# Block 0 of a fused attention and SwiGLU kernel: each half's reciprocal root on GpSimd, and two unread products in place of seven

## The chip, the cores and the metric

The kernel runs on one core of a Trainium2 chip. A core has five engines that run their own instruction streams and wait for each other through semaphores: TensorE (PE in the profile; its weight loads are PEld), VectorE (DVE), ScalarE (ACT), GpSimd (POOL) and SyncE (SP), which here only issues transfers. The metric is the device time of one execution in microseconds. The kernel before takes 1024.2 us, the median of three runs between 1023.02 and 1026.13.

## The reference, cut to what matters

```python
kv  = einsum('bhsd,bhse->bhde', k, v)             # 8 batches, 8 heads, 576 tokens, 64 wide
out = einsum('bhsd,bhde->bhse', q, kv)
rms = sqrt(mean(out * out, axis=-1) + 1e-06)      # one per token and head
x   = (out / rms * g_norm) as (4608 tokens, 512)
g   = x @ w_gate                                  # 512 x 1536
y   = (g * sigmoid(g) * (x @ w_val)) @ w_out      # back to 512
```

All of it is float32. The weights arrive as 64-bit words, which the kernel rounds to float32 itself, in pieces of 128 x 512.

## The kernel before, in words

The 4608 tokens are worked in nine blocks of 512 (`blocks`, an `Att` and an `Ffn` object for each). A block's attention gives x, transposed so that the model dimension lies across the partitions; then come the up products with silu, and the down product. While one block's down product runs, the attention of the next is fitted in between its steps (`Ffn.down` and its `fill`). Later blocks save multiplications with sums of sub-blocks (`Quad`, `Up`, `Inner`, `Down`), whose lines L565 and L728 are the bulk of TensorE's work. Block 0 is different: nothing runs ahead of it, its weights are still being loaded and rounded, and its up products are plain (`plain_up`, L1032).

The change is in how block 0 begins, `Att.first`. Its 512 tokens are two halves (i = 0 and 1) of two tiles of 128. The steps are these:

- `turn_q` transposes q on TensorE (L337) and copies it out of PSUM on VectorE (L341) and ScalarE (L339).
- `first_kv` makes kv of the first batch (L248).
- `heads` multiplies q with kv for one half (L361), into two PSUM tiles.
- `squares` squares them on ScalarE (L374) and sums over a head's 64 elements on VectorE (L375) into `z`. One half gives 16 numbers a partition.
- `root` makes 1/sqrt(z/64 + eps) on VectorE, for both halves at once: L381, a first guess from the bits (L384), and three Newton steps of L391, L392 and L393, eleven instructions on 128x32.
- `scale` multiplies the products by it (L113, two instructions a half).
- `turn_x` transposes the result on TensorE (L410), and ScalarE copies it out with the gain (L411) into x.
- `warm` has TensorE multiply something that nobody reads (L496), seven times, between the heads of half 1 and the transposes of x.

In between stands the rounding of the weights. `Words.begin` is ScalarE's absolute value (L146), VectorE's clamp (L147), sign (L152) and combination (L153); `Words.finish` is ScalarE's low part (L160) and VectorE's addition (L162). 36 pieces go through it; a piece's load waits for the buffer of the fourth piece before it, and so for L152 and L160 of that one. `plain_up` for feature group f needs the pieces 2f (gate) and 2f+1 (value) and runs group 0 in two halves of the tokens: the first needs x of half 0, the second x of half 1.

What sets the order on each engine: the framework puts the instructions into an order of its own, and `tc.issue_after` pins an instruction behind another. Each engine then runs its list strictly in order, so that one waiting instruction holds up everything behind it. In this kernel VectorE's list reads, from the sums of half 0: L147, L152, L153 of weight piece 0, sums of half 1, the eleven of the root, scaling of half 0, L162 of piece 0, scaling of half 1, piece 1.

Of the kernel before, what the change touches and what calls it, by code (L numbers as in the profile page):

```python
# [8 lines left out]
F32 = mybir.dt.float32  # L9
U32 = mybir.dt.uint32  # L10
I32 = mybir.dt.int32
OP = mybir.AluOpType
ACT = mybir.ActivationFunctionType

P = 128
# [3 lines left out]
def kernel(  # L19
# [41 lines left out]
    nc = tc.nc  # L61

    B, H, S, D = q.shape
# [7 lines left out]
    NS = DM // P  # L71
# [4 lines left out]
    eps = 1e-6  # L76
# [3 lines left out]
    def pool(name, bufs, **kw):  # L80
        return ctx.enter_context(tc.tile_pool(name=name, bufs=bufs, **kw))

    consts = pool("consts", 1)
    ld_pool = pool("ld", 4)
    st_pool = pool("st", 2)
# [8 lines left out]
    a_psum = pool("a_psum", 1, space=PS)  # L94
    b_psum = pool("b_psum", 3, space=PS)
# [6 lines left out]
    gain = consts.tile([P, 1], F32, name="gain")  # L102
    for u in range(2):
        nc.gpsimd.dma_start(out=gain[u * D : (u + 1) * D], in_=g_norm.rearrange("(d o) -> d o", o=1))

    kvs = [consts.tile([P, NS, D], F32, name=f"kv{i}") for i in range(3)]

# [11 lines left out]
    class Words:  # L119
# [12 lines left out]
        def __init__(self, src, shape):  # L132
            self.raw = ld_pool.tile([P, LD], U32, name="ld")[:, 0 : 2 * BLK]
            dst = self.raw.rearrange("p (a b) -> p a b", a=shape[0])
            self.sent = nc.sync.dma_start(out=dst, in_=src)
            self.shape = shape
            self.begun = False
# [45 lines left out]
    def round_w(name, j):  # L183
        if name == "o":
            dst = wo[:, j : j + 1, :]
        else:
            dst = wviews[name][0][j // 2][:, :, P * (j % 2) : P * (j % 2 + 1)]
        piece = words.pop((name, j))
        if not piece.begun:
            piece.begin()  # L190
        return piece.finish(dst)

    class Att:


        def __init__(self, n):
            self.n = n

            self.cut, half = divmod(n, 2)
            self.split = half * D  # L200
            self.ps, self.z = {}, None
            self.q, self.k, self.v, self.room = [], {}, {}, None
            self.halves = []
            self.quarters = n > 0

        def parts(self, t):

            n, first = self.n, P * t - D * self.n
            if t < self.cut:
                return [(n - 1, S + first, 0, P)]  # L210
            if t == self.cut and self.split:
                return [(n - 1, S - D, 0, D), (n, 0, D, P)]
            return [(n, first, 0, P)]
# [153 lines left out]
        def squares(self, i):  # L367
# [4 lines left out]
            for u in range(2):  # L372
                sq = self.sq[:, 2 * i + u]
                self.squared = nc.scalar.activation(out=sq, in_=self.ps[i][u], func=ACT.Square)  # L374
                self.summed = nc.vector.tensor_reduce(out=self.z[:, i, u], in_=sq, axis=mybir.AxisListType.X, op=OP.add)  # L375

        def root(self, i, k=1):


            z = self.z[:, i : i + k]  # L380
            nc.vector.tensor_scalar(out=z, in0=z, scalar1=1.0 / D, scalar2=eps, op0=OP.mult, op1=OP.add)  # L381
            self.y, a = (st_pool.tile([P, 2, 2, 2, NS], F32, name=x) for x in "ya")
            y, a = self.y[:, i : i + k], a[:, i : i + k]
            nc.vector.tensor_scalar(  # L384
                out=y.bitcast(I32), in0=z.bitcast(I32), scalar1=-0.5, scalar2=float(0x5F3759DF),
                op0=OP.mult, op1=OP.add,
            )
            flat = lambda t: t.rearrange("p i u t j -> p (i u t j)")
            y, a, z = flat(y), flat(a), flat(z)
            for _ in range(3):  # L390
                nc.vector.scalar_tensor_tensor(out=a, in0=y, scalar=-0.5, in1=y, op0=OP.mult, op1=OP.mult)  # L391
                nc.vector.tensor_tensor(out=a, in0=a, in1=z, op=OP.mult)  # L392
                nc.vector.scalar_tensor_tensor(out=y, in0=a, scalar=1.5, in1=y, op0=OP.add, op1=OP.mult)  # L393
# [72 lines left out]
        def first(self):  # L466
            self.turn_q(0, (b_psum, c_psum))
            self.first_kv(0, (b_psum, c_psum))
            last = self.first_kv(1, (b_psum, a_psum))

            with tc.issue_after(last.ins):
                self.heads(0, (0, 1), (m_psum, m_psum))
            with tc.issue_after(self.multiplied.ins):
                self.heads(0, (2, 3))
            self.squares(0)
            with tc.issue_after(self.multiplied.ins):
                self.turn_q(1, (b_psum, c_psum))

            with tc.issue_after(self.copied_q.ins), tc.issue_after(self.summed.ins):
                begun = words[pieces[0]].begin()  # L480
            with tc.issue_after(begun.ins):
                self.product(1, (b_psum, a_psum))
            self.warm()
            self.root(0, 2)
            self.scale(0)
            with tc.issue_after(self.squared.ins), tc.issue_after(self.scaled.ins):
                weights(1)
            self.turn_x(0)
            self.scale(1)
            return self.squared, self.scaled  # L490

        def warm(self):

            ps = c_psum.tile([P, NS, P], F32, name="c")
            for _ in range(7):
                nc.tensor.matmul(ps, lhsT=ident, rhs=self.qt[:, 3], start=True, stop=True)  # L496

        def turn(self):
# [553 lines left out]
    def load_weights(upto):  # L1052
        nonlocal loaded, sent
        while loaded < min(upto, len(pieces)):
            load_w(*pieces[loaded])
            loaded += 1
            if loaded == len(pieces) - NP:
                sent = words[pieces[loaded - 1]].sent

    def weights(upto):  # L1060
        nonlocal rounded
        while rounded < min(upto, len(pieces)):
            load_weights(rounded + 4)
            round_w(*pieces[rounded])
            rounded += 1
# [106 lines left out]
```

## Time and profile before

| | before |
|---|---|
| time, median of three runs | 1024.2 us |
| span of the profiled execution | 1021.4 us |
| TensorE busy | 1006.0 us, 98% |
| VectorE busy | 701.1 us, 69% |
| ScalarE busy | 227.9 us, 22% |
| GpSimd busy | 369.0 us, 36% |
| the unread products (L496) | from 20.67 us, 6.28 us |
| the root on VectorE (L381 to L393) | 23.26 to 25.73 us |
| first transposes of x (L410) | from 27.16 us |
| second token half of group 0 (L1032) | from 33.72 us |
| VectorE busy from 40 to 80 us | 40.00 of 40 us |
| GpSimd idle between the gain's load and the first sub-block difference | until 105.78 us |

How to read it: times are in microseconds from the span's start. A line of the timeline has start, duration, engine, source line, operation, tiles written and read, shapes, and how many instructions were merged into it; in brackets stands how long the engine was idle before it and what ended that. A float32 matmul is shown as two passes, so seven products are x14. L111, L112 and L113 are the helper lines for add, subtract and multiply, and carry many different operations; the tiles tell them apart.

### The profile page before, as it was taken

The page shows a single profiled execution, that of the slowest core. Times are in us where ns is not written, and L with a number is a line of the kernel's source. Part 1 is how long each engine was busy: PE and PEld are TensorE (multiplying, and loading weights), DVE is VectorE, ACT ScalarE, POOL GpSimd, SP SyncE. Part 2 cuts the span into 40 slices and gives each one's busy share as a digit, 9 for nine tenths or more (in the row PEclk, how much of TensorE's full clock was granted, in tenths as well). Part 3 has the DMA queues.
Part 4 walks back from the last instruction along what each step waited for, and adds up shares of the span by engine and source line. Part 5 has one row for each costly group of instructions (what it writes and reads, how often), then busy time and mean ns, then how long its engine had stood idle before and what let it go on. Part 6 is the DMA issues. An engine that isn't in the chain of part 4 may idle for free.

```text
span 1021.4 us, 21409 instructions
## 1 busy us (share of the span) xinstructions
PE 1006.0 (98%) x8522; PEld 897.1 (88%) x8522; DVE 701.1 (69%) x1169; ACT 227.9 (22%) x353; POOL 369.0 (36%) x280
## 2 busy tenths in 40 slices
PE   6999999999999999999999999999999999999998
PEld 4544688888999989998999899988998999989997
DVE  2999688998665946685558566665669466946661
ACT  2765112121211221121121211111121211221110
POOL 0000263534055503561246315630555045513670
PEclk9999999999999999999999999999999999999999
DMA  8689643767888377845686568636772766066601
GB/s 237 203 255 271 124 77 108 187 165 156 250 210 255 60 176 203 252 92 129 209 238 144 96 195 247 177 60 201 231 199 46 177 195 190 22 167 201 191 27 42
DMA packets 273845, 170.26 MB, mean 167 GB/s; under 512 B 150609, under 2 KB 241873, under 8 KB 273745
## 3 DMA queue, kind: packets, MB, share of 16 engines
q1 hardware_dynamic: 238800, 164.42, 59.3%
q10 hardware_dynamic: 34880, 4.46, 2.7%
q8 instruction: 68, 1.11, 0.4%
q14 instruction: 33, 0.26, 0.1%
q0 software_dynamic: 64, 0.00, 0.0%
HBM read 138.02 MB, written 22.41 MB: 157 GB/s over the span
## 4 chain that ended last, share of the span: by engine, by line
PE 90%; DVE 6%; DMA 2%; issue 1%; ACT 1%; SPq 0%; DVEq 0%; ACTq 0%
PE b L728 26%; PE b L565 19%; PE c L728 13%; PE c L565 10%; PE a L728 6%; PE a L565 5%; PE b L1032 4%; PE c L1032 4%; PE m L316 2%; PE m L361 1%; DVE r L112 1%; DVE xi L112 1%; DVE r L111 1%; DMA h<-in_v_dram 1%; DVE t L112 1%
## 5 line engine op out<-in xcount | busy, mean ns | idle before, releaser
L111 POOL TENSOR_TENSOR r<-r 128x256 f32<-128x256 f32 (+1 forms) x105 | 110.8, 1061 | 300.9 <-DVE r L111 272.2
L111 DVE TENSOR_TENSOR r<-b,r 128x512 f32<-128x512 f32 (+1 forms) x273 | 161.9, 606 | 65.5 <-PE b L728 60.1
L112 POOL TENSOR_TENSOR t<-wo 128x512 f32<-128x512 f32 x81 | 114.5, 1438 | 212.4 <-DVE wo L111 102.9
L111 DVE TENSOR_TENSOR r<-c,r 128x512 f32<-128x512 f32 (+1 forms) x179 | 108.5, 617 | 89.0 <-PE c L728 54.8
L728 PE MATMUL b<-x,t 128*128 128x128 f32 x1092 | 151.3, 276 | 0.0
L111 DVE TENSOR_TENSOR r<-a,r 128x512 f32<-128x512 f32 (+1 forms) x99 | 62.5, 631 | 113.4 <-PE a L565 70.7
L728 PEld LDWEIGHTS b<-x,t 128*128 128x128 f32 x1092 | 136.5, 192 | 0.8
L728 PE MATMUL c<-xi,t 128*128 128x128 f32 x840 | 112.4, 276 | 0.4 <-DVE xi L111 0.4
L113 POOL TENSOR_TENSOR h<-r 128x1024 f32<-128x1024 f32 (+1 forms) x40 | 82.3, 2072 | 76.9 <-DVE r L111 73.9
L728 PEld LDWEIGHTS c<-xi,t 128*128 128x128 f32 x840 | 102.9, 192 | 0.5 <-DVE xi L111 0.5
L565 PE MATMUL b<-wo,h 128*128 128x256 f32 x432 | 100.1, 383 | 0.1
L565 PE MATMUL b<-t,h 128*128 128x256 f32 x432 | 96.9, 381 | 0.0
L565 PEld LDWEIGHTS b<-t,h 128*128 128x128 f32 x432 | 81.6, 190 | 11.3 <-issue 0.2
L565 PEld LDWEIGHTS b<-wo,h 128*128 128x128 f32 x432 | 79.9, 190 | 13.1 <-DVE h L113 2.5
L742 ACT COPY r<-b 128x512 f32<-128x512 f32 x63 | 36.9, 585 | 211.6 <-PE b L728 211.6
L728 PE MATMUL b<-xi,t 128*128 128x128 f32 x588 | 79.8, 276 | 0.0
L728 PEld LDWEIGHTS b<-xi,t 128*128 128x128 f32 x588 | 72.4, 192 | 0.0
L728 PE MATMUL b<-x,wg 128*128 128x128 f32 x336 | 52.7, 279 | 0.2 <-DVE x L112 0.2
L728 PE MATMUL b<-x,wv 128*128 128x128 f32 x336 | 51.4, 276 | 0.0
L565 PE MATMUL a<-wo,h 128*128 128x256 f32 x216 | 48.3, 379 | 0.0
L565 PE MATMUL c<-t,s 128*128 128x256 f32 x216 | 48.1, 380 | 0.0
L565 PE MATMUL c<-wo,h 128*128 128x256 f32 x216 | 48.1, 379 | 0.0
(133 smaller groups left out, 1565.7 us busy)
## 6 DMA issues: line engine op xcount, KB each, us to landing
t<-w SPq DMA_DIRECT2D x336, 256.0 KB, 3.6
out_dram<-r SPq DMA_DIRECT2D x17, 512.0 KB, 3.1
ld<-in_k_dram SPq DMA_DIRECT2D x26, 288.0 KB, 5.2
ld<-in_v_dram SPq DMA_DIRECT2D x26, 288.0 KB, 5.9
ld<-in_moe_w_gate_dram SPq DMA_DIRECT2D x12, 512.0 KB, 4.8
ld<-in_moe_w_val_dram SPq DMA_DIRECT2D x12, 512.0 KB, 4.7
ld<-in_moe_w_out_dram SPq DMA_DIRECT2D x12, 512.0 KB, 4.9
w<-t SPq DMA_DIRECT2D x18, 256.0 KB, 3.0
```

Of the source, the lines that this page charges most:

```text
L111: add = lambda e, o, a, b: e.tensor_tensor(out=o, in0=a, in1=b, op=OP.add)
L112: sub = lambda e, o, a, b: e.tensor_tensor(out=o, in0=a, in1=b, op=OP.subtract)
L113: mul = lambda e, o, a, b: e.tensor_tensor(out=o, in0=a, in1=b, op=OP.mult)
L316: nc.tensor.matmul(self.kv_ps[r][u * D : (u + 1) * D, g, :], lhsT=k[:, u, c, :], rhs=v[:, u, c, :], start=(c == 0), stop=(c == KT - 1),)
L361: self.multiplied = nc.tensor.matmul(self.ps[i][u][p : p + D, t, j, :], lhsT=self.qt[rows, 2 * i + t, j, p : p + D], rhs=kvs[b % 3][rows, ...
L565: nc.tensor.matmul(banks[e][:, e], lhsT=lhsT, rhs=rhs, start=first and i == 0 and (e == 0 or banks[0] is not banks[1]), stop=i == self.ste ...
L728: nc.tensor.matmul(ps[:, i, f], lhsT=self.weight(o, p, f), rhs=self.operand(o, p), start=first and (i, f) == (0, 0), stop=True, skip_group ...
L742: nc.scalar.copy(out=dst, in_=ps)
L1032: nc.tensor.matmul(t, lhsT=w[f // 2][:, i, P * (f % 2) : P * (f % 2 + 1)], rhs=x[:, i, of], start=(i == 0), stop=(i == NS - 1),)
```

## The change: a root for each half on GpSimd

Instead of one root for both halves on VectorE, each half gets its own on GpSimd as soon as its sums are there: `power` does the multiply and add in one instruction and raises the result to the power -0.5, elementwise against a constant tile `half`. Its purpose is that half 0 can be scaled, and then transposed, without waiting for the sums of half 1, and that VectorE is rid of eleven instructions. The order in `first` follows: scaling of half 0 is pinned behind the begun weight piece 0, the heads of half 1 no longer wait for that piece, the first weight piece is finished and the sums of half 1 are done behind the scaling of half 0, and the second weight piece (`weights(2)`) is begun behind the sums of half 1. As the wait is meant to be shorter, `warm` makes two unread products and not seven. `root` stays for the later blocks.

The lines it adds stand at the places of before plus 2 (from L105), plus 9 (from L377) and so on; the numbers in the text are those of before.

```diff
+    half = consts.tile([P, 4 * NS], F32, name="half")
+    nc.gpsimd.memset(half, -0.5)
...
+        def power(self, i):
+            y = self.y = self.y or st_pool.tile([P, 2, 2, 2, NS], F32, name="y")
+            z, y = (x[:, i].rearrange("p u t j -> p (u t j)") for x in (self.z, y))
+            nc.gpsimd.tensor_scalar(out=z, in0=z, scalar1=1.0 / D, scalar2=eps, op0=OP.mult, op1=OP.add)
+            nc.gpsimd.tensor_tensor(out=y, in0=z, in1=half, op=OP.pow)
...
             self.squares(0)
+            self.power(0)
             with tc.issue_after(self.multiplied.ins):
                 self.turn_q(1, (b_psum, c_psum))
 
             with tc.issue_after(self.copied_q.ins), tc.issue_after(self.summed.ins):
                 begun = words[pieces[0]].begin()
             with tc.issue_after(begun.ins):
-                self.product(1, (b_psum, a_psum))
+                self.scale(0)
+            first = self.scaled
+            with tc.issue_after(self.copied_q.ins):
+                self.heads(1, range(NS), (b_psum, a_psum))
             self.warm()
-            self.root(0, 2)
-            self.scale(0)
-            with tc.issue_after(self.squared.ins), tc.issue_after(self.scaled.ins):
+            with tc.issue_after(first.ins):
                 weights(1)
+                self.squares(1)
+            self.power(1)
             self.turn_x(0)
+            with tc.issue_after(self.squared.ins), tc.issue_after(self.summed.ins):
+                weights(2)
             self.scale(1)
             return self.squared, self.scaled
...
-            for _ in range(7):
+            for _ in range(2):
                 nc.tensor.matmul(ps, lhsT=ident, rhs=self.qt[:, 3], start=True, stop=True)
```

More of the change, by code (lines that the diff above doesn't have):

```diff
@@ L200, in __init__ @@
             self.split = half * D
-            self.ps, self.z = {}, None
+            self.ps, self.z, self.y = {}, None, None
             self.q, self.k, self.v, self.room = [], {}, {}, None
```

## The prediction

> **What bounds the kernel now.** I read the page's busy times first, then TensorE's waits by stretch, then the timeline of block 0's start.
>
> ```profile
> PE 1006.0 (98%) x8522; PEld 897.1 (88%) x8522; DVE 701.1 (69%) x1169; ACT 227.9 (22%) x353; POOL 369.0 (36%) x280
> ```
>
> TensorE is busy 98% of the span, so only what shortens its work or its waits moves the end. Its waits between 20 and 200 us come to 0.9 us:
>
> ```profile
> PE b L1032 <- ACT x L411: 0.5, 2, 0.3
> PE m L410 <- DVE r L113: 0.2, 1, 0.2
> PE c L565 <- DVE r L111: 0.2, 1, 0.2
> ```
>
> That looks like nothing to gain, but the timeline of TensorE shows why: one real wait is filled.
>
> ```profile
> 20.67 6.28 PE L496 MATMUL c<-r,ident 128*128 128x512 f32 x14
> 27.16 1.07 PE L410 MATMUL m<-ident,r 128*128 128x128 f32 x8 [0.21 <-DVE r L113]
> 28.57 1.99 PE L1032 MATMUL b<-x,wg 128*128 128x256 f32 x8 [0.34 <-ACT x L411]
> ...
> 33.72 1.99 PE L1032 MATMUL b<-x,wg 128*128 128x256 f32 x8 [0.20 <-ACT x L411]
> 35.55 1.89 PE L1032 MATMUL c<-x,wv 128*128 128x256 f32 x8
> ```
>
> L496 is the seven products that nobody reads (two passes each), 6.28 us. TensorE really waits there for VectorE's chain:
>
> ```profile
> 21.96 1.27 DVE L375 TENSOR_REDUCE z<-r 128x8 f32<-128x512 f32 x2
> 23.26 0.18 DVE L381 TENSOR_SCALAR z<-z 128x32 f32<-128x32 f32 x1
> ...
> 25.50 0.19 DVE L393 SCALAR_TENSOR_TENSOR y<-a,y 128x32 f32<-128x32 f32 x1
> 25.73 1.29 DVE L113 TENSOR_TENSOR r<-m,y 128x512 f32<-128x512 f32 x2
> 26.93 0.68 DVE L162 CUSTOM_DVE_ANT_0 wg<-r 128x1024 uint16<-128x1024 uint16 x1
> 27.53 0.68 DVE L113 TENSOR_TENSOR r<-b,y 128x512 f32<-128x512 f32 x1
> ```
>
> Sums of both halves, root (23.26 to 25.73), scaling of half 0, transposes. From 33.72 on TensorE has no gap until past 105 us. What makes 33.72 earlier makes the end earlier, as long as VectorE and the transfers follow.
>
> **What the skill says.** Four places. (1) GPSIMD Engine Reference, 3.1 Elementwise: 2.6 cycles an element for a two-input operation, 4497 ns at 2048. The trace agrees: GpSimd's 128x1024 takes 2364 ns, 128x256 736. (2) The same page, 7 Performance pitfalls: 4 cycles an element for each link of a dependent fp32 chain; no run here shows it, and no page prices a power. (3) SBUF — State Buffer, two separate sides: GpSimd and those VectorE instructions that use the shared ports lock each other out for a whole instruction. The trace fits loosely: 128x512 takes GpSimd 1438 ns (t<-wo) against 1271 (h<-s,h). (4) TensorE: Matmul & The Clock Gate, part 1: about 3.4 us without work halves the clock. The granted clock here is 1.00 in every stretch up to 160 us.
>
> **Part by part.** The changed kernel, built but not run, gives each engine's order; durations come from the trace. VectorE's step from start to start is 0.60 us for a 128x512 L113, L153, L162 or a sum L375 (27.53 to 28.13), 0.33 for L147 or L152 (20.54 to 20.87). Line numbers are those of before.
>
> Removed from VectorE: the 11 root instructions, 23.26 to 25.73, 2.47 us. Removed from TensorE: five products of 0.86 us; the remaining two end near 23.0, before anything waits for them, so neither removal nor remainder costs anything.
>
> Added: per half, two GpSimd instructions on 128x16. The first (multiply, add) I put at 0.2 us, as GpSimd's 128x128 set-up operation takes 0.30 and a line through 128x256 (736 ns) and 128x1024 (2364 ns) gives about 0.23 at 16 elements. The power, p, is not in this trace. Lower end: no dearer than the add, 0.2. Upper end: an estimate from the second place above; were it 30 dependent steps (the number is mine), 16 elements x 30 x 4 cycles at the page's 1.2 GHz is 1.6 us. I take 0.7, nearer the lower end because operations on separate elements can overlap. The constant tile of -0.5 is one small memset near 3 us, when GpSimd is idle until 105: free.
>
> Half 0. The sums end at 20.62. Hops between engines are about 0.08 (0.14 to TensorE): the power starts near 20.95 and y is there at 21.03+p. Meanwhile VectorE does the three instructions L152, L147, L153 of the first weight piece; L147 waits for ScalarE, where the piece's L160 now stands ahead of the copy L339 and moves L146 from 19.70 to 20.17. So L153 ends its turn at 21.98. Scaling starts at S = max(21.98, 21.03+p) = 21.98, in place of 25.73: with p under 0.95 this root is hidden.
>
> Half 1. VectorE's order after S: two scalings, L162 of piece 0, two sums (end S+3.07), L147 and L152 of piece 1, then it waits for the second power. Behind that wait stand both scalings of half 1 and the end of weight piece 1, and TensorE waits for both. y arrives at S+3.07+0.08+0.2+0.05+p+0.08: A = S+3.48+p = 26.16. Filler covers to S+3.67, so about 0.5 us of it is idle. This is the wait the change adds.
>
> TensorE after A: the scalings take to A+1.88, transposes from A+2.02; piece 1 ends at A+2.48, the first c product starts at A+2.66 and its four take 1.83 (31.41 to 33.24); three remaining transposes 0.33. The second b group starts at A+4.85 = 31.01, against 33.72. TensorE gains 2.7. ScalarE could bind instead: from its first L411 to the copies of half 1 it took 5.15 (27.83 to 32.98), table load included; from S+2.1 that is ready at 29.9, so it doesn't.
>
> What VectorE gains matters too, as the weights' rounding keeps it full (20.00 of 20 us, 40 to 80), and loads wait for it. Its order puts L162 of piece 3 at A+6.2 = 32.36 (34.77 before); then the wait for ScalarE's L146 of piece 5 and two differently placed instructions leave the next weight pair at A+10.84 = 37.0 against 39.11: 2.1 us. At 119 us block 1's q lands behind that chain:
>
> ```profile
> 117.27 1.24 DVE L331 STREAM_TRANSPOSE r<-ld 128x1024 f32<-128x1024 f32 x1
> 119.20 1.25 DVE L331 STREAM_TRANSPOSE r<-ld 128x1024 f32<-128x1024 f32 x1 [0.70 <-DMA ld<-in_q_dram]
> ```
>
> The second ends at 120.44, and TensorE's L361, begun at 120.55, needs it after some 0.2 us. So TensorE can keep VectorE's 2.1 plus about 0.25 of slack, not the whole 2.7. I take off nothing more for locked ports than rounds it to 2.3, as VectorE's L147 and L153 run beside both powers and could cost a few tenths. 1024.2 - 2.3 = 1021.9.
>
> **Rivals.** (a) The power costs what an add does, p = 0.2, and q is early enough: A = 25.66, second b at 30.51, 3.2 gained: 1021.0. For: 16 elements are next to nothing. Against: the line above is for adds, and VectorE's share is 0.6 less. (b) The gain is there at 31 us and is given back: q's 32 small loads, issued from 98.2 to 117.5, don't move with VectorE, and only the slack, 0.25, plus what moves of it, say 0.4, stays; or TensorE, idle from S+4.6 = 26.6 to A+2.02 = 28.2, drops its clock and takes 1.7 more (half of a 3.4 us window): 1023.6. For: transfer share 0.95 from 80 to 92 us. Against: the issues of weights waited 42.1 us for VectorE's L152 between 36 and 98, so they move with it; and 1.6 us idle is less than a window. (c) The power is long, a routine of 100 steps as by the estimate above, p = 5: S = 26.03, A = 34.51, second b at 39.36, 5.6 later than before: 1029.8, slower. It becomes the bound twice, once per half, as the second waits behind the first's scaling; the loss begins at p = 2.2. For: no row shows a power. Against: nothing in the trace.
>
> **How the numbers follow.** Forecast 0.50, rival (a) 0.20, (b) 0.13, (c) 0.17. 0.3% is 3.1 us. Of the forecast 0.10 passes it (p and the slack both on the good side), 0.40 stays within; (a) counts as faster, (b) as same, (c) as slower: 0.30, 0.53, 0.17. The low end is (a) with 0.8 for the spread of the times (1023.02 to 1026.13): 1020.2. The high end takes in p = 1.6 (S = 22.63, A = 27.71, 1.2 gained, 1023.0) and (b), with the same spread and more, since p may run past 2: 1025.0. (c) is left out.
>
> **What would show it.** GpSimd's power of 128x16 beginning near 20.95 and lasting about 0.7; the first scaling near 22.0; the first sum of half 1 near 23.8; VectorE idle about 0.5 us before the scaling of half 1, released by GpSimd; the second b group near 31.0; a small wait, if any, of L361 for L331 near 118 us; TensorE's clock still 1.00. Powers over 2.2 us, a lower clock near 28, or L361 waiting over a microsecond for q would prove me wrong.

## The result and the profile after

The changed kernel takes 1027.85 us (median of 4 runs, 1027.20 to 1030.21) against 1023.68 for the kernel before (4 runs, 1023.02 to 1026.13): a ratio of 1.0038, 95% interval 1.0020 to 1.0055. It is slower by about 4 us where 2.3 us of gain were forecast, and above 1025.0, the highest time that was allowed for. The profiled executions span 1025.8 and 1021.4 us.

Line numbers are now those of the changed kernel: L383 and L384 are the power's multiply-add and the power, L377 the sums, L115 the scaling, L419 the transposes of x, L1047 the plain up products, L511 the unread products, L333 and L363 the transposes of block 1's q and its products with kv. E2 has the line numbers of the kernel before; E4, F1 and F4 add lines of their own, so that theirs differ by a few from those of the kernel they start from.

The first line of the page shows how little a share of busy time tells: TensorE is at 98% as before.

```profile
PE 1004.3 (98%) x8512; PEld 896.9 (87%) x8512; DVE 699.3 (68%) x1158; ACT 228.2 (22%) x353; POOL 375.5 (37%) x285
```

TensorE's waits between 20 and 200 us (engine, line, who ended them; us in total, times, longest) do tell. Where 0.9 us stood, 6.5 stand, and nearly all of it is one line, the transposes of x waiting for the scaling:

```profile
PE m L419 <- DVE r L115: 5.6, 2, 3.7
PE c L580 <- DVE r L113: 0.3, 1, 0.3
PE b L1047 <- ACT x L420: 0.3, 1, 0.3
PE m L363 <- DVE r L333: 0.3, 1, 0.3
```

The scaling in turn waits for GpSimd. This is GpSimd's timeline (start, duration, engine, line, operation, tiles, shapes, and in brackets the idle time before and what ended it):

```profile
20.50 0.30 POOL L383 TENSOR_SCALAR z<-z 128x16 f32<-128x16 f32 x1 [17.46 <-DVE z L377]
20.88 2.93 POOL L384 TENSOR_TENSOR y<-z,half 128x16 f32<-128x16 f32 x1
27.01 0.31 POOL L383 TENSOR_SCALAR z<-z 128x16 f32<-128x16 f32 x1 [3.20 <-DVE z L377]
27.40 2.95 POOL L384 TENSOR_TENSOR y<-z,half 128x16 f32<-128x16 f32 x1
```

A power of 128x16 takes 2.93 and 2.95 us. The multiply-add on the same 16 elements takes 0.30. VectorE works for 1.1 us of the first power and for 0.2 of the second, and the two differ by 0.02 us; in F1 below VectorE does nothing during the power, and an element is nearly as dear (5.47 us for 32, 0.17 each, against 0.18). So sharing ports with VectorE isn't what makes it long. VectorE's timeline shows both waits:

```profile
21.83 0.69 DVE L155 SCALAR_TENSOR_TENSOR r<-r 128x512 uint32<-128x512 uint32 x1
23.84 1.29 DVE L115 TENSOR_TENSOR r<-m,y 128x512 f32<-128x512 f32 x2 [1.32 <-POOL y L384]
...
25.65 1.27 DVE L377 TENSOR_REDUCE z<-r 128x8 f32<-128x512 f32 x2
...
30.39 0.69 DVE L115 TENSOR_TENSOR r<-b,y 128x512 f32<-128x512 f32 x1 [2.79 <-POOL y L384]
```

And TensorE's timeline shows what they cost:

```profile
21.45 1.98 PE L511 MATMUL c<-r,ident 128*128 128x512 f32 x4
25.28 1.06 PE L419 MATMUL m<-ident,r 128*128 128x128 f32 x8 [1.85 <-DVE r L115]
26.68 1.99 PE L1047 MATMUL b<-x,wg 128*128 128x256 f32 x8 [0.34 <-ACT x L420]
32.42 1.30 PE L419 MATMUL m<-ident,r 128*128 128x128 f32 x5 [3.75 <-DVE r L115]
33.51 3.62 PE L1047 MATMUL c<-x,wv 128*128 128x256 f32 x8
36.93 0.85 PE L419 MATMUL m<-ident,r 128*128 128x128 f32 x3
37.57 2.30 PE L1047 MATMUL b<-x,wg 128*128 128x256 f32 x8
```

Half 0 is early, as meant: its transposes start at 25.28, 1.9 us sooner than before. Half 1 is late: after 3.75 us of idle time its transposes start at 32.42, and the second b group, at 33.72 before, starts at 37.57. A second loss shows in the durations. Eight passes of c took 1.99 us in the kernel before and take 3.62 here. The table by stages says why (window, span, busy time of each engine, then the granted clock of TensorE, the transfers' share and GB/s). First one row of the kernel before, then four of the changed one:

```profile
30.00:35.00 5.00, 4.71 (x25) 3.72 (x24) 5.00 (x12) 4.97 (x9) 0.00 (x0) 1.00 0.75 233
```

```profile
25.00:30.00 5.00, 3.06 (x16) 2.29 (x16) 2.60 (x6) 4.04 (x6) 2.91 (x2) 1.00 0.27 84
30.00:35.00 5.00, 2.58 (x9) 2.34 (x10) 4.62 (x10) 1.82 (x4) 0.35 (x1) 0.66 0.16 46
35.00:40.00 5.00, 5.00 (x18) 4.10 (x18) 2.72 (x6) 2.19 (x4) 0.00 (x0) 0.66 0.64 207
40.00:45.00 5.00, 5.00 (x17) 2.91 (x16) 4.77 (x11) 4.24 (x9) 0.00 (x0) 1.00 0.71 215
```

The clock records of the trace put it exactly: half clock from 31.56 us for 6.83 us. TensorE's 2.58 busy us between 30 and 35 us, all from 32.42 on, are half-speed work as well.

### The profile page after: what moved, and what is told of

It reads as the page before. It is cut to its first block, busy times and chain, and to the rows that moved or that the text cites. A ratio compares the mean times of both kernels' runs of the same rounds, so it can differ in the third digit from the quotient of the medians.

```text
span 1025.8 us, 21387 instructions
## 1 busy us (share of the span) xinstructions
PE 1004.3 (98%) x8512; PEld 896.9 (87%) x8512; DVE 699.3 (68%) x1158; ACT 228.2 (22%) x353; POOL 375.5 (37%) x285
## 4 chain that ended last, share of the span: by engine, by line
PE 84%; DVE 9%; DMA 3%; SPq 1%; issue 1%; POOL 1%; ACT 0%; DVEq 0%; ACTq 0%
PE b L743 26%; PE b L580 20%; PE c L743 13%; PE c L580 10%; PE a L743 6%; PE a L580 5%; DVE r L155 1%; PE m L363 1%; PE m L318 1%; SPq L286 1%; DVE xi L114 1%; DVE r L149 1%; DVE r L154 1%; DMA h<-in_v_dram 1%; DMA ld<-in_v_dram 1%
## 5 line engine op out<-in xcount | busy, mean ns | idle before, releaser
L115 POOL TENSOR_TENSOR h<-r 128x1024 f32<-128x1024 f32 (+1 forms) x40 | 82.3, 2073 | 78.1 <-DVE r L113 74.3
```

The lines of the kernel that those rows point to most:

```text
L115: mul = lambda e, o, a, b: e.tensor_tensor(out=o, in0=a, in1=b, op=OP.mult)
```

## The experiments

Profiles of different executions can't be laid on each other from the span's start: the first products of block 0 (heads of half 0) begin between 15.3 and 17.2 us, as their loads land. So the table counts from that first product, and gives the difference to the kernel before, each from one profiled execution. "To the last" runs to TensorE's last instruction; L363's wait is block 1's wait for q; "idle" is TensorE's longest pause between its unread products and the second b group; the clock column says how long TensorE had half clock before its last instruction. The last column is the median time against that of the kernel before in the same comparison (1023.68 for the change itself, then 1024.07 for E1 to E4 and 1024.11 for F1, F3 and F4). The 64 products counted from took 2.33 us in the first four profiles of the table and 1.91 to 2.20 in the others, so a difference of under half a microsecond says nothing here.

| kernel | second b group | wait of L363 | to the last | idle | half clock | median time |
|---|---|---|---|---|---|---|
| before | 18.06 us | 0 | 1002.42 us | 0.34 | 0 | |
| changed | +3.98 | 0.25 | +4.53 | 3.75 | 6.83 | +4.17 |
| E1 changed, seven unread | +4.68 | 0 | +5.42 | 2.89 | 3.41 | +3.76 |
| E2 before, two unread | +2.14 | 0.76 | +2.97 | 4.49 | 6.83 | +2.06 |
| E3 changed, multiply | -3.14 | 1.42 | -1.55 | 1.06 | 0 | -1.97 |
| E4 changed, ScalarE's root | -1.66 | 0 | -1.56 | 1.47 | 0 | -1.43 |
| F1 before, one power | +6.52 | 0.69 | +7.76 | 3.66 | 6.83 | +4.95 |
| F3 changed, nine unread | +2.20 | 0.71 | +3.71 | 0.51 | 0 | +3.06 |
| F4 before, ScalarE's root | -1.01 | 0 | -0.80 | 0.34 | 0 | -0.69 |

Theory after the result: the power's 2.94 us is twice on the path, once for each half, and the pause it makes in TensorE then halves the clock. Rivals: the clock alone, because five unread products went; the new order of VectorE by itself; a fixed charge for each GpSimd instruction rather than the power.

### E3: everything but the power

```diff
-            nc.gpsimd.tensor_tensor(out=y, in0=z, in1=half, op=OP.pow)
+            nc.gpsimd.tensor_tensor(out=y, in0=z, in1=half, op=OP.mult)
```

> The changed kernel with a multiplication in place of the power, so it scales by the wrong number and leaves the root out; the order of instructions on all five engines is the same. It takes the 2.93 us of the power down to about 0.2 to 0.3 and leaves every wait and hop. Theory (the prediction's chain was right and only the power's size was off): first scaling near 22.0, second token half of group 0 near 30.6 to 30.9, TensorE at full clock throughout, about 1021.3, 2.4 faster than before. Rival (the new waits or the order of weights and loads cost something of their own, such as q of block 1 arriving late near 119 us): the early part is as said but the time ends at 1023 or more.

Measured: 1022.10 us (1020.75 to 1026.21, 19 runs), ratio 0.9982, interval 0.9975 to 0.9989. The order, the waits and the two unread products are those of the change; only the power is gone. GpSimd's timeline, same instructions in the same places:

```profile
20.28 0.30 POOL L383 TENSOR_SCALAR z<-z 128x16 f32<-128x16 f32 x1 [17.26 <-DVE z L377]
20.66 0.22 POOL L384 TENSOR_TENSOR y<-z,half 128x16 f32<-128x16 f32 x1
25.00 0.31 POOL L383 TENSOR_SCALAR z<-z 128x16 f32<-128x16 f32 x1 [4.12 <-DVE z L377]
25.39 0.27 POOL L384 TENSOR_TENSOR y<-z,half 128x16 f32<-128x16 f32 x1
```

What follows: the operation makes the whole loss and more; neither the hand-over to GpSimd nor the order nor the missing unread products loses anything when the operation is short. TensorE's waits between 20 and 200 us show the second thing this run tells:

```profile
PE m L419 <- DVE r L115: 1.5, 2, 1.1
PE m L363 <- DVE r L333: 1.4, 1, 1.4
```

Of the 3.1 us won at the second b group, 1.4 are given back at the first products of block 1, which wait for q. VectorE, which transposes q, was early, and itself waited for q's load:

```profile
118.16 1.25 DVE L333 STREAM_TRANSPOSE r<-ld 128x1024 f32<-128x1024 f32 x1 [2.38 <-DMA ld<-in_q_dram]
```

In the profile before, the same instruction began at 119.20 after 0.70 us of waiting for the same load (the prediction shows the line). Counted from the first product, VectorE was ready 2.5 us sooner in E3, and the load came only 0.9 sooner: SyncE began to issue block 1's q at 95.81 in place of 98.21 us, but took 20.68 us over it in place of 19.26. So the limit is q's load, and not VectorE's chain as the prediction had it.

### E1: the seven unread products back

```diff
-            for _ in range(2):
+            for _ in range(7):
```

> The changed kernel with seven unread products, as in the kernel before, in place of two; nothing else. Theory: half of the loss is TensorE's clock. In the changed kernel TensorE stands idle from 28.7 to 32.4 us behind the second power and then runs at half clock until about 38.3. With seven products the transposes of half 0 move from 25.3 to about 27.6, the idle stretch before half 1 shrinks from 3.75 to about 2.1 us, the clock stays full, and the second token half of group 0 starts near 36.0 in place of 37.6: about 1026.0, some 1.8 faster than the changed kernel, still 2.3 slower than before. Rival: the power alone is the loss and the clock only goes with it; then filling an idle stretch gives nothing: 1027.9, or later by what the products delay.

Measured: 1027.83 us (1026.43 to 1029.42, 7 runs), ratio 1.0037, interval 1.0026 to 1.0048. My expectation missed: 1026.0 with a full clock. The unread products stand before the transposes of half 0; the long pause is between the halves:

```profile
29.21 1.99 PE L1047 MATMUL b<-x,wg 128*128 128x256 f32 x8 [0.34 <-ACT x L420]
34.09 3.40 PE L1047 MATMUL c<-x,wv 128*128 128x256 f32 x8 [2.89 <-DVE wv L164]
37.33 1.04 PE L419 MATMUL m<-ident,r 128*128 128x128 f32 x8
38.71 1.99 PE L1047 MATMUL b<-x,wg 128*128 128x256 f32 x8 [0.34 <-ACT x L420]
```

TensorE still pauses for 2.89 us, and in this execution its clock is half from 33.58 for 3.41 us. The runs of this one kernel divide by their mean clock: two at 0.998 span 1027.1 and 1027.6 us, five at 1.000 span 1024.6 to 1027.2, median 1025.3. So the same program loses the clock in some executions and not in others (that the pause was as long in those without a trace is assumed); the difference of the medians is about 2 us, from two executions on one side. And without the drop it is still about 3 us above the kernel before (41 runs at 1.000, median span 1022.2): the power alone makes this order slower.

### F3: nine unread products

```diff
-            for _ in range(2):
+            for _ in range(9):
```

> The changed kernel with nine unread products in place of two: the powers stay as long, TensorE waits about 1.2 us instead of 3.75 (2.9 with seven). Theory (the power costs about 2 us of path by itself, the halved clock the other 1.7 or so): the clock stays full, second group of b about 15.3 us after the first unread product (after 16.12, with seven 16.99), time about 1026.1. Rival (the clock adds nothing to the time, the power alone explains 3.8 us): time 1027.8 as with seven. Rival (the clock explains nearly all): time near 1024.5.

Measured: 1027.17 us (1025.86 to 1028.48, 8 runs), ratio 1.0030, interval 1.0019 to 1.0040. The clock stays full until TensorE has ended in the profile and at a mean of 1.000 in six of eight runs, and the kernel stays slow: a full clock does not save it, so the rival that gave the clock nearly all is out. The one that gave it nothing isn't excluded by this run, since E1, to which it compares, kept the clock in five of seven runs too; it falls by the comparison of the change with E3 below. My own number missed by 1.1 us. The second b group is where I put it, or earlier (14.89 us after the first unread product, 15.3 expected); behind it, block 1 waits 0.71 us for q, and pauses of TensorE between 150 and 260 us come to 1.59 us against 0.80 before and 0.93 to 1.43 in the other profiles. I had counted the path up to the second b group only. The runs don't say why those later pauses grew. In E1 and F3 the framework also puts all of half 1's transposes behind the c group, so that in F3 the second b group follows the scaling by 37.48 - 31.66 = 5.8 us and not by the prediction's 4.85; E1 and F3 are therefore no pure measure of the clock's share in the change.

### E2: the kernel before with two unread products

```diff
-            for _ in range(7):
+            for _ in range(2):
```

> The kernel before with two unread products in place of seven; the root stays on VectorE. Theory (the clock falls when TensorE is idle too long): TensorE is idle from about 22.4 to 27.2 us, 4.8 us, then runs at half clock for some 5 to 6 us; the second token half of group 0 starts near 36 in place of 33.7: about 1026.0. Rival (unread products are without use, as nothing waits for them): 1023.7, the same as before.

Measured: 1026.13 us (1024.32 to 1027.28, 13 runs), ratio 1.0018, interval 1.0010 to 1.0026, as expected. The scaling isn't later for it, and still TensorE's timeline reads:

```profile
21.46 1.98 PE L496 MATMUL c<-r,ident 128*128 128x512 f32 x4
27.93 1.94 PE L410 MATMUL m<-ident,r 128*128 128x128 f32 x8 [4.49 <-DVE r L113]
29.80 3.57 PE L1032 MATMUL b<-x,wg 128*128 128x256 f32 x8
```

The clock is half from 26.19 for 6.83 us: b takes 3.57 us where it took 1.99. This is the price of a pause behind an unchanged chain: products that nobody reads hold the clock up, worth 2 us here. One other thing differs: all eight transposes of half 1 now follow the c group, where seven stood ahead of it. By the steps at full clock that order would not have made the second b group later (an estimate: 1.83 + 1.72 + 1.38 = 4.9 us from the first b group to the second, 5.15 in the kernel before; E2 takes 6.5). Runs with one window of half clock (mean 0.998, five, median span 1023.2) and with two (0.996 to 0.997, eight, 1024.55) lie 1.35 us apart.

### F1: one power for both halves, in the order of before

```diff
-            self.root(0, 2)
+            self.power()
```

with `power` as in the change, but once over 128x32; the seven unread products stay.

> Before's order with one GpSimd power over both halves (128x32) in place of the 2.47 us root on VectorE; seven unread products stay. If the power's time grows with its elements (2.95 us at 128x16, so about 5.9 at 128x32): scaling of half 0 starts 3.9 us later, TensorE idles about 3.9 us after the unread products and its clock halves, second group of b 17 us or more after the first unread product (before 13.05, after 16.12), time about 1024 + 3.9 + 1.5 to 3 = 1029.4 to 1031. If the power is a fixed charge for the instruction (about 3.0 us): scaling 1.0 us later, idle about 1.3 us, clock stays full, second group of b at 14.0, time about 1025.0, and one power for both halves would have cost less than two.

Measured: 1029.06 us (1028.47 to 1031.29, 5 runs), ratio 1.0057, interval 1.0045 to 1.0070. GpSimd's and TensorE's timelines:

```profile
24.34 0.21 POOL L384 TENSOR_SCALAR z<-z 128x32 f32<-128x32 f32 x1 [21.28 <-DVE z L378]
24.64 5.47 POOL L385 TENSOR_TENSOR y<-z,half 128x32 f32<-128x32 f32 x1
```

```profile
31.57 1.94 PE L420 MATMUL m<-ident,r 128*128 128x128 f32 x8 [3.66 <-DVE r L116]
33.44 3.78 PE L1042 MATMUL b<-x,wg 128*128 128x256 f32 x8
```

Twice the elements, 5.47 us for 2.94: 2.53 us for 16 more, 0.158 us an element, which leaves 2.94 - 16 x 0.158 = 0.4 for the instruction. The fixed charge is out; the price is in the elements, and dividing the power in two halves costs only the 0.4 once more. The time is just under the 1029.4 that growth with the elements was to give at least.

### E4: the change with the root on ScalarE

```diff
-            nc.gpsimd.tensor_scalar(out=z, in0=z, scalar1=1.0 / D, scalar2=eps, op0=OP.mult, op1=OP.add)
-            nc.gpsimd.tensor_tensor(out=y, in0=z, in1=half, op=OP.pow)
+            nc.scalar.activation(out=z, in_=z, func=ACT.Sqrt, scale=1.0 / D, bias=half[:, 0:1])
+            nc.vector.reciprocal(out=y, in_=z)
```

The constant tile holds eps, and one unused Sqrt at the start loads ScalarE's table early.

> The changed kernel with the root of each half as ScalarE's square root (of the sum over 64 plus eps) and VectorE's reciprocal, two unread products; ScalarE's first table is made to hold the square root by one dummy square root at the start. Theory: from the sums of a half to its scaling some 0.7 to 1.2 us in place of 3.4; first scaling near 22.4, scaling of half 1 near 27.4, second token half of group 0 near 32.2, about 1022.2, 1.5 faster than before. Rival: ScalarE's list, in which the square root stands behind copies and weight work, or a second table load of 1.28 us, eats the gain: 1023.7 or more.

Measured: 1022.64 us (1021.36 to 1024.04, 17 runs), ratio 0.9989, interval 0.9982 to 0.9996: 1.4 us faster than the kernel before and 5 faster than the change. ScalarE's root of 128x16 takes 0.31 us and VectorE's reciprocal 0.25, in place of 2.94, and no further table load appears in ScalarE's timeline. TensorE's timeline:

```profile
24.52 1.06 PE L420 MATMUL m<-ident,r 128*128 128x128 f32 x8 [0.45 <-DVE r L116]
25.93 1.99 PE L1048 MATMUL b<-x,wg 128*128 128x256 f32 x8 [0.34 <-ACT x L421]
29.39 1.97 PE L1048 MATMUL c<-x,wv 128*128 128x256 f32 x8 [1.47 <-DVE wv L165]
```

So the order by halves does what it is for once the root is short, and with two unread products: the pause of 1.47 us leaves the clock full, and no run's mean clock is below 0.999.

### F4: the order of before with the root on ScalarE

```diff
-            self.root(0, 2)
+            self.power()
...
-            for _ in range(7):
+            for _ in range(5):
```

with `power` made of ScalarE's Sqrt and VectorE's reciprocal on 128x32, as in E4.

> Before's order, one root for both halves, but by ScalarE's Sqrt (0.31 us on 128x16) and VectorE's reciprocal (0.25 us on 128x16) in place of the 11 instructions of 2.47 us; five unread products instead of seven so that they end before they are in the way. If the price of the root alone is what can be won, without splitting or reordering: scaling 1.1 to 1.8 us earlier, second group of b 11.3 to 11.9 us after the first unread product (before 13.05), clock full, time 1022.3 to 1023.0. If the order by halves is what wins: no better than 1023.7.

Measured: 1023.42 us (1022.41 to 1026.02, 13 runs), ratio 0.9997, interval 0.9989 to 1.0005: not told apart from the kernel before, and neither of the two times expected. VectorE's timeline has the chain as short as expected:

```profile
22.81 1.27 DVE L379 TENSOR_REDUCE z<-r 128x8 f32<-128x512 f32 x2
24.47 0.35 DVE L386 RECIPROCAL y<-z 128x32 f32<-128x32 f32 x1 [0.39 <-ACT z L385]
24.86 1.29 DVE L117 TENSOR_TENSOR r<-m,y 128x512 f32<-128x512 f32 x2
```

From the end of the sums to the scaling 0.78 us pass, 2.50 before. But in the profiled execution q's second half was late: its transposes begin 4.2 us after the first product, 2.9 in the profile before, and the last sum ends 8.8 us after it, 7.6 before. With one root for both halves everything hangs on the later half. That may be why only 0.7 us of 1.7 shows; it is argued from one profile, not tested, and the profiled execution is the fastest of the thirteen, so it says little of what held back the median. Whether the order by halves beats this one stays open: the intervals of E4 and F4 overlap.

## Why the prediction was wrong, point by point

**The step that failed: "I take 0.7".** The power was bounded between 0.2 and 1.6 us, the upper end from 30 dependent steps of 4 cycles for each of 16 elements, with 30 a number of mine. It takes 2.94. By F1's 0.158 us an element, the same reckoning would have needed about 47 of those steps for each element. The lower end, that a power is no dearer than an add, is out by ten times even against the 0.30 of the multiply-add beside it; the reason for leaning to it, that operations on separate elements can overlap, is not borne out: from 16 to 32 elements the time nearly doubles. The cited place, the GPSIMD Engine Reference, 7 Performance pitfalls, prices one link of a dependent chain; nothing in it said how many links a power has, and I closed the range at a guess. Whether a power is such a chain at all, no run shows.

**The formulas around it held.** With p = 2.94, S = 21.03 + p = 23.97 and A = S + 3.48 + p = 30.39, in the time of the before profile. The changed profile's first product comes 0.13 us earlier; so 23.84 and 30.26 were due, and 23.84 and 30.39 are in the trace. The second b group at A + 4.85 would then be 1.5 us later than before. The stated break-even, p = 2.2, is right too: (2.94 - 2.2) x 2 = 1.5. Rival (c) named this case, "it becomes the bound twice, once per half", but at p = 5, and with 0.17 for it.

**The second failure, "1.6 us idle is less than a window".** This set the clock aside. The pause grew with the power to 3.75 us, and I had added the clock to no case with a long power. What it costs is read without any model from two kernels with the same instructions in the same order: from the start of half 1's transposes to the second b group, E3 takes 30.39 - 27.73 = 2.66 us and the change 37.57 - 32.42 = 5.15. The 2.5 us more are the half clock. Together with 1.5 from the power they make the 4.0 by which the second b group is later; the time is 4.2 longer. No run has the change's own order with the long power at full clock, so this division rests on the two profiles.

Nor was "less than a window" the right test. A pause of 2.89 us, shorter than one window, halved the clock in E1's profile, and E1's runs divide into those that lost it and those that didn't. The stretches of half clock are 3.41 us or twice that and begin 2.4 to 3.2 us into the pause (E1 33.58 - 31.20, F1 31.11 - 27.91); in the 3.41 us ahead of them TensorE had still worked for 0.2 to 1.0 us. The Trainium skill, TensorE: Matmul & The Clock Gate, part 1, says both that the clock falls after an idle window of about 3.4 us and that the window is free-running, with effects that vary from run to run. The runs agree with the second: in the clock records of the nine traces every stretch between two changes of the clock is a whole multiple of 3.413 us (6.827 is two, 13.653 four, 1003.518 is 294). The first, taken as the least pause that matters, which is how I used it, they contradict (2.89 us). Where else the clock falls stays open: its mean was 0.997 or 0.998 in three of E3's 19 runs and 0.998 in three of the 45 of the kernel before beside it, and these runs have no trace.

**"Neither removal nor remainder costs anything"** was said of the unread products. With a short root it holds: with two products E3 and E4 keep the clock in their profiles, E4 in all 17 runs and E3 in 16 of 19. With a long pause ahead of the transposes it doesn't: E2 loses 2.1 us by removing five of them. But they weren't the cause of this loss either, since putting them back (E1) changes little: they stand ahead of half 0, and the pause is ahead of half 1.

**What q lets through** was right in that q's transposes come to bind, and wrong in what holds them. With an operation of 0.22 to 0.27 us, rival (a)'s value, the second b group comes 3.1 us earlier (3.2 worked out) and 1.4 of that is lost again at block 1's q, so that (a)'s 1021.0 isn't reached: E3 takes 1022.1. The prediction let q move with VectorE's chain, 2.1 us, though its own line showed the second transpose waiting 0.70 us for the load. In E3 that wait grew to 2.38: VectorE moved by 2.5 and the load by 0.9. Rival (b)'s first half had this, that q's loads don't move with VectorE; counted as before, their first issue did move by 2.2, but their last only by 0.8. What lengthened the issuing, the runs don't say. So E3's gain of 2.0 beside the forecast's 2.3 is near by luck, not by the reason given.

## What to carry to other kernels

An operation whose kind no row of the profile shows has no upper bound until it is measured: find the value at which the change begins to lose (here 2.2 us, worked out in advance) and ask what evidence excludes it. If none does, that case needs more than a corner of the chances. And a wait added ahead of TensorE is to be counted with the clock: a wait that costs 1.5 us by the chain cost 4 here, and work that nobody reads can be worth its time.

## What the runs showed of the hardware

- GpSimd's elementwise power in float32: 2.93 to 3.14 us for 128x16, 5.47 for 128x32; 0.158 us an element and 0.4 for the instruction. Both figures are worked out from these two sizes. A multiply in its place takes 0.22 to 0.27, the multiply-add ahead of it 0.30 for 128x16 and 0.21 for 128x32, so a tenth of a microsecond isn't to be read; ScalarE's Sqrt 0.31 (0.32 for 128x32), VectorE's reciprocal 0.25 (0.35).
- TensorE lost half its clock in profiles with pauses of 2.89, 3.66, 3.75 and 4.49 us, and kept it with 0.51, 1.06 and 1.47. It stayed low for 3.41 or 6.83 us, though work came again within 0.5 to 1.7 us of the fall.
